# Two elementwise products of an RWKV-6 and MLP-mixer kernel, given from VectorE to GpSimd

## The chip, the cores and the metric

The kernel runs on one core of one Trainium2 chip. A core has five engines with a queue of instructions each: TensorE (PE in the profile; its weight loads are PEld), VectorE (DVE), ScalarE (ACT), GpSimd (POOL) and SyncE (SP), which here issues the DMAs. The metric is the time of one execution on the device in microseconds; the median of three runs before the change is 521.4 us (519.96 to 521.54).

## The reference

A linear recurrence over 768 time steps feeds a token mixer and a channel mixer, all in float32. Batch B = 4, heads H = 8, steps S = 768, head size D = 48.

```python
for t in range(S):                                   # attention block
    cur = np.einsum('bhd,bhe->bhde', u[None] * kt, vt)
    y[:, :, t] = np.einsum('bhd,bhde->bhe', rt, state + cur)
    state = wt[:, :, :, None] * state + np.einsum('bhd,bhe->bhde', kt, vt)
x = y.transpose(0, 2, 1, 3).reshape(B, S, H * D)
h = np.maximum(x.transpose(0, 2, 1) @ w_tok1, 0.0) @ w_tok2      # 768 -> 256 -> 768
z = x + h.transpose(0, 2, 1)
out = z + np.maximum(z @ w_ch1, 0.0) @ w_ch2                     # 384 -> 1536 -> 384
```

What matters for the change is the term with `u`: a step's own key counts in its own output, weighted by `u`. For a step and a head it is one number, the sum over the 48 places of a head of r times k times u.

## The kernel before, in words

The recurrence is worked in chunks of 64 steps. A *unit* is 256 steps of one batch for all heads; there are twelve (three for each batch). In a unit, VectorE forms running products of the decays by scans (`ends`, line 372, and `begins`, line 380), scales the keys (`keys`, line 377) and the queries (`queries`, line 383) with them; TensorE transposes the keys (`k_ps`, line 287), multiplies keys by queries to the weights of steps within a chunk (`gram`, line 257), makes each chunk's contribution to the state (`kv_ps`, line 303) and the outputs (`y_ps`, line 317 for what comes from the state and line 338 for what comes from within the chunk). VectorE masks the gram into the tile `at` (line 425) and advances the state (line 448), ScalarE scales the state (line 438).

The diagonal of `at`, a step's weight on itself, is made apart. Units 0 to 3 make it on TensorE. Units 4 to 11 make it from rows of tokens: a DMA (line 154) brings r and k of the unit's 256 steps side by side as the tile `near`, 128 partitions by 2 by (2 x 384); `products` multiplies r by k in place (line 400), then by `u` (line 402, `u_rows` holds u in all partitions), then sums over each head's 48 places (line 405); `sums_put` writes the 16 sums of a partition on the diagonal of `at` by a predicated copy (line 410), before the second part of `y_ps` is made. `near` has one buffer: the next unit's load follows the reduction of line 405 in the queue of SyncE, and waits for it.

The mixer of one batch is interleaved with the units of the next. The token mixer is `h_ps` (lines 522 and 529) with a transpose (line 537). The channel mixer's first product is made in blocks of 256 tokens, as fifteen products of thirds (`thirds`: `z_ps`, line 585, gathered by ScalarE at line 590, by VectorE at lines 593, 596 and 599, and cut at zero by ScalarE at line 602); its second product in seven products of halves (`quarters`: `q_ps`, lines 642 and 646, gathered at lines 655 to 684, with sums of `z` at lines 689 and 690). For the first batch plain products take the place of some of these (lines 547 and 624).

The order of work is written out by hand. `woven` merges lists of steps by their weights, and the function `strict` then binds the instructions of TensorE, VectorE, ScalarE and, in part, SyncE to that order, each within its own engine's queue. GpSimd is not among the engines so bound; before the change it has only a few memsets and selects at the start, and a load and branches at the end. The dependencies between engines are semaphores that the framework puts in from the tiles read and written.

In the middle batches the three steps of `products` are woven with the first ten steps of `thirds`, in the function `middle_mixing`; in the first mixing they stand one by one between the steps of the unit, in `steps`.

Of the kernel before, what the change touches and what calls it, by code (L numbers as in the profile page):

```python
# [20 lines left out]
DM = H * D  # L21
T = 64
C = S // 128
UC = 2
# [38 lines left out]
def rwkv6_then_mixer(  # L63
# [18 lines left out]
    pe, dve, act, pool, sp = nc.tensor, nc.vector, nc.scalar, nc.gpsimd, nc.sync  # L82
# [35 lines left out]
    u_rows = const.tile([128, DM], f32, name="u_rows")  # L118
# [227 lines left out]
    def unit(i):  # L346
# [50 lines left out]
        def products(n):  # L397
            t = nears[i]
            if n == 0:
                dve.tensor_mul(t[:, :, 0], t[:, :, 0], t[:, :, 1])  # L400
            elif n == 1:
                dve.tensor_mul(t[:, :, 0], t[:, :, 0], u_rows.unsqueeze(1).to_broadcast([128, UC, DM]))
            else:
                L["sums"] = apool.tile([128, UC, H], f32, name="sums")
                dve.tensor_reduce(out=L["sums"], in_=nears.pop(i)[:, :, 0].rearrange("p c (h e) -> p c h e", e=D),
                                  axis=mybir.AxisListType.X, op=ALU.add)
# [58 lines left out]
        def each(f, n):  # L465
            return [lambda m=m: f(m) for m in range(n)]

        return dict(ranges=each(ranges, 2), ends=ends, keys=keys, begins=begins, queries=queries, own_u=each(own_u, A),
                    own_gram=own_gram, copied=each(copied, UC), taken=each(taken, 3),
                    own_put=own_put, products=[lambda n=n: products(n) for n in range(3)], sums_put=sums_put,  # L470
                    tokens=tokens, gram=gram, mask=mask, carry=carry, before=before, seen=seen, after=after,
                    scaled=[lambda c=c, j=j: scaled(c, j) for c in range(UC) for j in range(2)],
# [354 lines left out]
    for bt in range(B):  # L827
        ahead = []
        if bt == 0:
            to_ch = [single(e, n) for n, e in enumerate(to_ch)]  # L830
            both = [f for e in zip(ups[0], ups[1]) for f in e]
            b, t = [turned[0]] + turned[1:10:2], turned[2:12:2] + turned[11:]
# [127 lines left out]
```

## Time and profile before

| | |
|---|---|
| median of three runs | 521.4 us |
| the profiled execution's own time | 518.61 us |
| its span, first to last instruction | 516.9 us |
| granted TensorE clock, mean | 0.989 |
| TensorE busy | 490.1 us (95%) |
| VectorE busy | 388.4 us (75%), 633 instructions |
| ScalarE busy | 229.2 us (44%) |
| GpSimd busy | 1.3 us, 10 instructions |
| near loads, line 154 | 8 of 768 KB, 4.1 to 5.6 us from issue to landing |

The span is what the profile covers, and the profiled execution's own time is 1.7 us longer; that execution was quicker than the median of the three runs. Busy times are sums over one engine's instructions and say nothing alone on what sets the end: the chain of waits does, and the idle time of an engine that is named there.

### The profile page before, as it was taken

How to read it: one execution, taken by the hardware profiler on the slowest of the kernel's cores; microseconds unless marked ns; L12 is line 12 of the kernel's file. 1: busy time of each engine (PE TensorE's matmuls, PEld its weight loads, DVE VectorE, ACT ScalarE, POOL GpSimd, SP SyncE). 2: the span in 40 equal slices, each digit the busy share in tenths (PEclk: the TensorE clock that was granted, in tenths of full speed). 3: DMA queues.
4: the chain of work that ended last, by engine and by line, in shares of the span. 5: the costliest groups of instructions: out<-in, count | busy, mean ns of one | idle time of the engine just before them, and what ended most of it. 6: DMA issues, size and time to landing. Idle time of an engine off the chain costs nothing.

```text
span 516.9 us, 13327 instructions
## 1 busy us (share of the span) xinstructions
PE 490.1 (95%) x5794; PEld 427.7 (83%) x5794; DVE 388.4 (75%) x633; ACT 229.2 (44%) x533; POOL 1.3 (0%) x10
## 2 busy tenths in 40 slices
PE   3589999899999999999999999999999999999996
PEld 2476687666789768999999868999999859999996
DVE  7999969959895878967779668987858616684653
ACT  3967675564453435434325445524335414531300
POOL 0000000000000000000000000000000000000000
PEclk9789999999999999999999999999999999999999
DMA  8845954443342442121212522100000000000000
GB/s 298 324 168 163 276 176 149 155 152 93 115 113 79 149 134 62 63 73 63 70 54 64 164 74 63 61 33 0 3 32 1 18 15 1 1 2 34 1 32 34
DMA packets 20946, 46.06 MB, mean 89 GB/s; under 512 B 2129, under 2 KB 13009, under 8 KB 20881
## 3 DMA queue, kind: packets, MB, share of 16 engines
q1 hardware_dynamic: 20736, 45.14, 27.6%
q8 instruction: 47, 0.77, 0.6%
q14 instruction: 19, 0.15, 0.1%
q10 hardware_dynamic: 144, 0.00, 0.0%
HBM read 40.41 MB, written 4.72 MB: 87 GB/s over the span
## 4 chain that ended last, share of the span: by engine, by line
PE 74%; DVE 16%; ACT 5%; issue 3%; DMA 1%; DVEq 0%
PE z_ps L585 18%; PE q_ps L646 12%; PE q_ps L642 11%; PE h_ps L529 6%; PE h_ps L522 6%; PE h_ps L624 5%; PE z_ps L547 3%; PE gram L257 2%; PE y_ps L317 2%; PE y_ps L338 2%; DVE w L380 2%; DVE to_end L372 2%; PE kv_ps L303 2%; PE xT_ps L537 2%; DVE z L593 2%
## 5 line engine op out<-in xcount | busy, mean ns | idle before, releaser
L438 ACT ACTIVATE before<-state,to_end 112x48 f32<-112x48 f32 x176 | 44.5, 324 | 65.0 <-DVE state L448 60.7
L590 ACT COPY z<-z_ps 128x512 f32<-128x512 f32 x54 | 30.6, 587 | 57.4 <-PE z_ps L585 39.5
L593 DVE TENSOR_TENSOR z<-z,z_ps 128x512 f32<-128x512 f32 x54 | 35.9, 683 | 24.5 <-PE z_ps L585 15.9
L547 PE MATMUL z_ps<-xT,wch 128*128 128x256 f32 x216 | 48.3, 381 | 0.9 <-DVE wch L227 0.9
L602 ACT ACTIVATE z<-z 128x512 f32<-128x512 f32 x54 | 33.3, 631 | 33.1 <-DVE z L593 29.0
L547 PEld LDWEIGHTS z_ps<-xT,wch 128*128 128x128 f32 x216 | 40.4, 190 | 6.9 <-DVE wch L227 1.3
L646 PE MATMUL q_ps<-wch,z 128*128 128x192 f32 x222 | 43.3, 331 | 0.0
L642 PE MATMUL q_ps<-wch,z 128*128 128x192 f32 x222 | 42.8, 329 | 0.2
L642 PEld LDWEIGHTS q_ps<-wch,z 128*128 128x128 f32 x222 | 36.5, 190 | 0.9 <-ACT z L602 0.6
L646 PEld LDWEIGHTS q_ps<-wch,z 128*128 128x128 f32 x222 | 36.5, 190 | 0.6
L529 PE MATMUL h_ps<-h,wtok 128*128 128x384 f32 x96 | 34.9, 492 | 0.6 <-ACT h L524 0.6
L596 DVE TENSOR_TENSOR z<-z,z_ps 128x512 f32<-128x512 f32 x45 | 30.0, 683 | 7.0 <-PE z_ps L585 6.5
L624 PE MATMUL h_ps<-wch,z 128*128 128x384 f32 x96 | 33.3, 494 | 1.4 <-DVE wch L227 1.4
L522 PE MATMUL h_ps<-x,wtok 128*128 128x384 f32 x96 | 33.1, 491 | 0.0
L531 DVE TENSOR_TENSOR x<-x,h_ps 128x384 f32<-128x384 f32 x24 | 13.2, 551 | 24.4 <-PE h_ps L529 24.4
L585 PE MATMUL z_ps<-rk,wch 128*128 128x128 f32 x256 | 31.2, 275 | 0.0
L585 PEld LDWEIGHTS z_ps<-rk,wch 128*128 128x128 f32 x256 | 30.0, 192 | 0.0
L372 DVE TENSOR_TENSOR_SCAN to_end<-w,starts 112x1041 f32<-112x1041 f32 (+1 forms) x13 | 28.1, 2159 | 2.1 <-DMA w<-in_w_dram 1.7
L380 DVE TENSOR_TENSOR_SCAN w<-w,starts 112x1041 f32<-112x1041 f32 x12 | 27.8, 2320 | 0.0
L624 PEld LDWEIGHTS h_ps<-wch,z 128*128 128x128 f32 x96 | 17.5, 190 | 12.4 <-DVE wch L227 2.0
L646 PE MATMUL q_ps<-scratch,z 128*128 128x192 f32 x144 | 27.7, 329 | 0.0
L642 PE MATMUL q_ps<-scratch,z 128*128 128x192 f32 x144 | 27.4, 327 | 0.0
(181 smaller groups left out, 912.6 us busy)
## 6 DMA issues: line engine op xcount, KB each, us to landing
rk<-in_rk_dram SPq DMA_DIRECT2D x36, 192.0 KB, 3.7
near<-in_near_dram SPq DMA_DIRECT2D x8, 768.0 KB, 4.3
w<-in_w_dram SPq DMA_DIRECT2D x11, 520.5 KB, 3.7
vt<-in_v_dram SPq DMA_DIRECT2D x12, 384.0 KB, 3.8
out_dram<-o SPq DMA_DIRECT2D x24, 192.0 KB, 1.9
spare<-in_w_ch_dram SPq DMA_DIRECT2D x8, 512.0 KB, 4.9
scratch<-in_w_ch_dram SPq DMA_DIRECT2D x8, 512.0 KB, 4.8
rk<-in_rk_dram SPq DMA_DIRECT2D x6, 512.0 KB, 8.5
```

The source lines that it names most:

```text
L372: dve.tensor_tensor_scan(to, of, start, 0.0, op0=ALU.mult, op1=ALU.add)
L380: dve.tensor_tensor_scan(w_[:ROWS], w_[:ROWS], starts[:ROWS], 0.0, op0=ALU.mult, op1=ALU.add)
L438: act.mul(t[:ROWS, a], state[bt, g][:ROWS, a], by_last(c, j)[:, a:a + 1])
L522: pe.matmul(sums[i], wtok1[:, c, ts(i, 128)], x_of()[:, c, :], start=(c == 0), stop=(c == C - 1))
L529: pe.matmul(ps, wtok2[:, i, ts(c, 128)], h1[:, i, :], start=(i == 0), stop=(i == DTOK // 128 - 1))
L547: pe.matmul(ps, wch1[:, m, ts(jt, 128)], xT[:, m, ts(s, SEG)], start=(m == 0), stop=(m == DM // 128 - 1))
L585: pe.matmul(ps[:, q], lefts[r][:, ts(q, 128)], of[r], start=first and q == 0, stop=end and q == JB - 1, skip_group_check=True)
L593: dve.tensor_add(to(n), to(n), ps)
L602: act.activation(to(n), to(n), AF.Relu)
L624: pe.matmul(ps, zs[s][:, jt, ts(n, 128)], wch2[:, jt, :], start=(jt == 0), stop=(jt == NJ - 1))
L642: pe.matmul(L["q"], a[:, j, :], b[:, j, :], start=(j == 0), stop=False)
L646: pe.matmul(L["q"], a[:, j, :], b[:, j, :], start=False, stop=(j == HJ - 1))
```

## The change

The two products of `products` are issued on GpSimd rather than on VectorE, for units 4 to 11. The reduction of line 405 stays on VectorE.

```diff
         def products(n):
             t = nears[i]
             if n == 0:
-                dve.tensor_mul(t[:, :, 0], t[:, :, 0], t[:, :, 1])
+                pool.tensor_mul(t[:, :, 0], t[:, :, 0], t[:, :, 1])
             elif n == 1:
-                dve.tensor_mul(t[:, :, 0], t[:, :, 0], u_rows.unsqueeze(1).to_broadcast([128, UC, DM]))
+                pool.tensor_mul(t[:, :, 0], t[:, :, 0], u_rows.unsqueeze(1).to_broadcast([128, UC, DM]))
             else:
                 L["sums"] = apool.tile([128, UC, H], f32, name="sums")
                 dve.tensor_reduce(out=L["sums"], in_=nears.pop(i)[:, :, 0].rearrange("p c (h e) -> p c h e", e=D),
                                   axis=mybir.AxisListType.X, op=ALU.add)
```

VectorE's queue has 16 instructions fewer, GpSimd's 16 more, in the order of the units; the other queues keep their instructions and their order. In GpSimd's queue the first product of a unit waits for the near load and for the earlier readers of the tile, the second for the first (in unit 4 also for the load of `u_rows`, line 722), and the reduction on VectorE now waits for GpSimd.

## Prediction

> **What bounds the kernel now.** I read the engines' shares first, then the chain that ended last, then what TensorE waited for in the stretch where the eight units run, and last the timeline around each near load.
>
> ```profile
> PE 490.1 (95%) x5794; PEld 427.7 (83%) x5794; DVE 388.4 (75%) x633; ACT 229.2 (44%) x533; POOL 1.3 (0%) x10
> ...
> PE 74%; DVE 16%; ACT 5%; issue 3%; DMA 1%; DVEq 0%
> ```
>
> The first line is the busy time of the engines, the second the chain by engine. TensorE is busy for 95% of the span and carries 74% of the chain; VectorE has a quarter of its time free. Of the chain's pieces from 100 to 430 us, none is at line 400 or 402. The reduction of line 405 is in it three times (165.4, 238.0 and 355.9 us), but it stays on VectorE. So the question is where TensorE waits for VectorE. The waits of TensorE's matmuls between 126 and 430 us are two lines:
>
> ```profile
> PE y_ps L317 <- ACT before L438: 0.6, 1, 0.6
> PE gram L257 <- DVE rk L383: 0.3, 2, 0.2
> ```
>
> The columns are the total in us, the number and the longest. In 304 us TensorE stands idle for 0.9 us. Nothing that makes VectorE faster here can give back more than that.
>
> **What is removed.** The two groups that leave VectorE, and the rows of GpSimd that come nearest to what it gets, by form:
>
> ```profile
> L402 DVE TENSOR_TENSOR near<-near,u_rows 128x768 f32<-128x768 f32 x8 | 7.6, 951 | 0.0
> L400 DVE TENSOR_TENSOR near<-near 128x768 f32<-128x768 f32 x8 | 7.6, 949 | 0.0
> ```
>
> ```profile
> L177 POOL TENSOR_SCALAR_AFFINE_SELECT strictly<-strictly 64x64 f32<-64x64 f32 x2 | 0.5, 236 | 0.1
> masks.py:199 POOL TENSOR_SCALAR_AFFINE_SELECT ident<-ident 128x128 f32<-128x128 f32 x1 | 0.3, 294 | 0.1
> ```
>
> VectorE loses 16 instructions of 0.95 us, 15.2 us of 388.4. Most of them ran into a wait of VectorE for somebody else: after line 400 at 229.44 it waits 2.42 us for z_ps, after line 402 at 160.25 0.58 us for q_ps, at 183 the later 0.87 us for h_ps. In the stretches without such a wait (203 to 207, 321 to 325 us) TensorE runs its thirds' products without a gap, so an earlier VectorE only waits longer. Gain taken: 0; bound: 0.9 us.
>
> **What GpSimd gets.** Eight times two products of 768 elements a partition, two operands from SBUF. The trace has no such instruction on GpSimd, so the price is bounded. From 64 to 128 elements the select grows by 58 ns, 0.91 ns an element over a base of 178 ns, reading one tile and writing one. At that slope 768 elements take 0.87 us, the low end. If the second operand is read after the first, the slope doubles: 178 + 768 x 1.81 = 1.57 us, which I take, as that is the select's row with one read more. If the write does not overlap either, three times the slope: 2.27 us, the high end.
>
> A page of the Trainium skill (GPSIMD Engine Reference, section 3.1) gives 4497 ns for a two-operand product of 2048 elements against 2293 ns on VectorE. An estimate from it is 1.69 us for 768, and the sum below would be some 0.5 us larger.
>
> **When it runs, and who waits.** GpSimd's queue is not under the hand-written order; its first product of a unit waits for the near load alone (and the tile's earlier readers), so it starts when the load lands, not where VectorE stood. Landings, from issue and time to landing, against the reduction that needs the result: 110.0/138.3, 144.6/165.3, 170.4/184.9, 190.3/206.9, 212.1/237.9, 243.1/269.6, 274.9/324.8, 330.1/355.8. The closest pair is 14.5 us apart, and two products at the high end with a hand-over take under 5 us. (The first unit's second product waits for u_rows, issued at 108.84 and landed 2.4 us later.) So the new wait of the reduction on GpSimd costs 0; if it did come late, the update of line 448 behind it, and the scaling and the product y_ps after it, would be next. Nothing else is in GpSimd's queue until the end, and the queue on SyncE keeps its order: the next near load still follows the reduction, at 184.9 and 206.9 up to 1.7 us earlier, as VectorE has less to do in front of it.
>
> **What it disturbs.** The trace shows no VectorE instruction with two SBUF operands beside a running GpSimd one (GpSimd's ten all lie in the first 2.1 us, beside a memset). The one end is that both run undisturbed, cost 0. The other is that VectorE stands still as long as GpSimd runs. I take the step between: one of the two waits for the other where both read two tiles in SBUF, and not where VectorE reads PSUM, since GpSimd touches no PSUM tile here.
>
> The Trainium skill (SBUF — State Buffer, "Who interferes with whom") says the same and speaks against this change: a VectorE instruction with two SBUF inputs and a GpSimd one that reads SBUF share a read interface, and the one that comes second blocks for the whole of the first; no run shown here can tell. Without it, only the odds between the ends would be more even.
>
> Site by site, two products of 1.57 us from the landing on. At 110 VectorE idles (4.70 us before line 628): 0. At 144.6 the weight sums and a scan are held by some 2.5 us, but keys (line 377) end at 149.7 for a transpose at 154.4, and 3.43 us of idle follow: 0. At 190.3 the predicated copy at 193.05 slips by under 1 us, with 2 us in hand before y_ps at 196.4; at 212 and 330 line 377 slips by under 1.5 us, with 4 us in hand; at 243 2.07 us of idle follow: 0 each. Two places are left.
>
> The first is at 275 us:
>
> ```profile
> 275.43 1.22 DVE L377 TENSOR_TENSOR rk<-rk,to_end 112x1024 f32<-112x1024 f32 x1
> ...
> 277.56 0.36 DVE L656 TENSOR_TENSOR o<-x,z 128x192 f32<-128x192 f32 x1 [0.91 <-ACT z L655]
> ...
> 277.84 2.32 DVE L380 TENSOR_TENSOR_SCAN w<-w,starts 112x1041 f32<-112x1041 f32 x1
> ...
> 282.06 1.22 DVE L383 TENSOR_TENSOR rk<-rk,w 112x1024 f32<-112x1024 f32 x1
> ...
> 283.33 1.26 PE L257 MATMUL gram<-rk 48*64 48x64 f32 x64 [0.17 <-DVE rk L383]
> ```
>
> Every line from 277.56 on is in the chain, and TensorE already waits at its end. With the load landed at 274.85, the first product runs from 274.95 to 276.52; line 377 starts 1.09 us late and ends at 277.74; the second product runs to 279.31; line 656 starts there instead of at 277.56, and all that follows is 1.75 us late. At 0.87 us a product it is 0.35, at 2.27 us 3.15.
>
> The second is at 170.4 us: the predicated copy (170.69) waits until 172.05, the second product runs from 173.25 to 174.82, line 673 starts at 174.82 instead of 172.26. Of these 2.56 us the waits of VectorE for q_ps (0.18 and 1.68) take most: the scan of the next unit starts 0.55 late, and with it keys, for which the transpose at 180.8 already waits: 0.5 us. By the ends of the price 0 and 2.
>
> Sum: 1.75 + 0.5 = 2.25 us on the profiled execution's span of 516.9 (its own time is 518.61). The median of the runs is 521.4, which gives 523.65, 0.43% more. With the ends of the price it is +0.35 to +5.15.
>
> **Rivals.** *No collision* (0.31): both engines read at once; VectorE is 15 us less busy, TensorE gets at most the 0.9 us back: 520.5 to 521.4. For it: nothing in the trace shows a shared thing. It decides if a VectorE product beside a GpSimd one keeps its 0.95 us. *VectorE stands still at every landing* (0.14), PSUM reads too: of 3.14 us at each, what the slack leaves is 1.3 at 170, 2.0 at 190, where y_ps already waits for before, 1.0 at 212 and 330, 1.1 at 243 and 2.2 at 275: +8.6, about 530. *The relief reaches TensorE by a way that the chain hides* (0.05), say a PSUM bank freed earlier: over 1.6 us, below 519.8; against it stand the 0.9 us. The likeliest case, my forecast, has 0.5.
>
> **Numbers.** A measurement of this kernel tells about 0.3%, 1.6 us, from no change. The forecast case passes that with some 0.36 of its 0.5 (a product over about 1.3 us); with the standstill, slower is 0.50. No collision and the rest make 0.45 within it, and 0.05 is faster. The range goes from 520.5 (all idle given back) to 526.5 (the forecast's upper end); most of the standstill and the hidden relief are left out, under 2 in 10. The forecast's own range is 521.7 to 526.5.
>
> **What would show it.** GpSimd has 16 products of 1.2 to 2 us, each pair begun within 0.5 us of a landing; VectorE's busy time falls by 15 us less what its rows beside them grow by; lines 377 and 380 near 275 us, or line 410 near 171, last longer or start later; gram waits near 283 us for line 383 by about 2 us rather than 0.2. The twin place near 400 us, with no load before it, stays as it is. It is wrong if those VectorE rows keep their times (no collision), if rows that read PSUM grow as well (standstill), or if a reduction waits for GpSimd.

## The result and the profile after

The changed kernel is slower: a ratio of 1.0049 to the kernel before, 95% interval 1.0039 to 1.0059, which is 2.5 us. Over 19 runs each the medians are 521.73 us after and 519.32 us before; the 521.4 us that the prediction started from was the median of three runs only, so the difference is to be compared, not the absolute time. The profiled execution of the changed kernel has a span of 520.0 us against 516.9, at a granted TensorE clock of 0.99.

The engines' busy time and the chain by engine, page of the changed kernel:

```profile
PE 491.6 (95%) x5794; PEld 428.3 (82%) x5794; DVE 386.0 (74%) x617; ACT 229.2 (44%) x533; POOL 38.7 (7%) x26
...
PE 72%; DVE 18%; ACT 4%; issue 4%; DMA 1%; SPq 0%; DVEq 0%; ACTq 0%
```

VectorE has 16 instructions fewer and yet is busy only 2.4 us less, and its share of the chain has grown from 16% to 18%. What TensorE's matmuls waited for between 126 and 434 us (total, number, longest, in us):

```profile
PE gram L257 <- DVE rk L383: 1.1, 2, 1.0
PE k_ps L287 <- issue: 0.8, 1, 0.8
PE y_ps L317 <- ACT before L438: 0.6, 1, 0.6
PE k_ps L287 <- DVE rk L377: 0.5, 1, 0.5
```

0.9 us of waits have become 3.0: line 383 is waited for longer, and the matmuls of the keys' transpose (`k_ps`), which are not in the table of before, wait for line 377 once by name (at 181.92) and once under "issue", where the profile names nobody: that one begins at 279.21, 0.1 us after line 377's end.

The place near 275 us in the timeline (start, length, instruction, idle time before it), GpSimd and VectorE:

```profile
276.12 0.68 DVE L596 TENSOR_TENSOR z<-z,z_ps 128x512 f32<-128x512 f32 x1
276.20 1.83 POOL L400 TENSOR_TENSOR near<-near 128x768 f32<-128x768 f32 x1 [28.18 <-DVE z L593]
...
276.72 2.39 DVE L377 TENSOR_TENSOR rk<-rk,to_end 112x1024 f32<-112x1024 f32 x1
...
278.10 2.95 POOL L402 TENSOR_TENSOR near<-near,u_rows 128x768 f32<-128x768 f32 x1
...
279.03 0.34 DVE L656 TENSOR_TENSOR o<-x,z 128x192 f32<-128x192 f32 x1
...
279.30 3.94 DVE L380 TENSOR_TENSOR_SCAN w<-w,starts 112x1041 f32<-112x1041 f32 x1
...
286.41 1.26 PE L257 MATMUL gram<-rk 48*64 48x64 f32 x64 [0.96 <-DVE rk L383]
```

Line 377 took 1.22 us before and 2.39 now: it ends about as long after the end of GpSimd's first product (278.03) as it needs for itself. GpSimd's second product is then the one that is held: its 2.95 us end at 281.05, 1.7 us after line 656 is over, and undisturbed it takes 1.81. And line 380, 2.32 us before and 3.94 now, waits for that: it ends 2.2 us after the product. Each waits for the other's end. Just ahead, at 276.12, the subtraction of line 596, which reads PSUM, keeps its 0.68 us beside the same first product.

The second place, at 171 us, first two lines of the kernel before, then the changed one:

```profile
172.26 0.36 DVE L673 TENSOR_TENSOR o<-o,z 128x192 f32<-128x192 f32 x1
172.54 0.68 DVE L511 TENSOR_TENSOR wch<-wch,spare 128x512 f32<-128x512 f32 x1
```

```profile
170.83 3.11 POOL L400 TENSOR_TENSOR near<-near 128x768 f32<-128x768 f32 x1 [19.17 <-DVE z L690]
171.00 1.30 DVE L410 COPY_PREDICATED at<-diagonal,sums 128x1024 f32<-128x1024 uint8 x1
...
172.57 1.59 DVE L673 TENSOR_TENSOR o<-o,z 128x192 f32<-128x192 f32 x1
...
174.02 1.81 POOL L402 TENSOR_TENSOR near<-near,u_rows 128x768 f32<-128x768 f32 x1
174.08 2.30 DVE L511 TENSOR_TENSOR wch<-wch,spare 128x512 f32<-128x512 f32 x1
...
181.92 1.09 PE L287 MATMUL k_ps<-ident,rk 128*128 128x128 f32 x8 [0.51 <-DVE rk L377]
```

Here the predicated copy keeps its time and GpSimd's first product is held behind it, although its recorded start is 0.17 us earlier: its end, 173.94, less 1.81 us is 172.13, about the copy's end. Then line 673 (0.36 us before) and line 511 (0.68 before) are held behind a product each.

A ledger comes from laying the start times of VectorE's instructions of the two timelines side by side (after minus before, in us):

| stretch | lag at its end | added in it |
|---|---|---|
| up to 54, ahead of the first product | 0.30 | 0.30 |
| unit 4's and 5's products, to 170 | 0.31 | 0.01 |
| unit 6's, to 188 | 1.04 | 0.73 |
| unit 7's and 8's, to 238 | 1.04 | 0.00 |
| unit 9's, to 260 | 1.29 | 0.25 |
| unit 10's, to 295 | 3.09 | 1.80 |
| unit 11's, to the end | 3.10 | 0.01 |

The products account for 2.8 us, at three places out of eight. The 0.30 us arise before any product; in the traces of the experiments this early lag is anything from -0.4 to 2.95 us, and it belongs to no theory.

### The profile page after: what moved, and what is told of

Its sections match the earlier page's. It is cut to its first block, busy times and chain, and to the rows that moved or that the text cites. A ratio compares the mean times of both kernels' runs of the same rounds, so it can differ in the third digit from the quotient of the medians.

```text
span 520.0 us, 13349 instructions
## 1 busy us (share of the span) xinstructions
PE 491.6 (95%) x5794; PEld 428.3 (82%) x5794; DVE 386.0 (74%) x617; ACT 229.2 (44%) x533; POOL 38.7 (7%) x26
## 4 chain that ended last, share of the span: by engine, by line
PE 72%; DVE 18%; ACT 4%; issue 4%; DMA 1%; SPq 0%; DVEq 0%; ACTq 0%
PE z_ps L585 18%; PE q_ps L646 12%; PE q_ps L642 11%; PE h_ps L529 6%; PE h_ps L624 5%; PE h_ps L522 5%; PE z_ps L547 3%; PE gram L257 3%; DVE w L380 2%; PE y_ps L317 2%; PE y_ps L338 2%; DVE to_end L372 2%; PE kv_ps L303 2%; PE xT_ps L537 2%; DVE rk L377 1%
## 5 line engine op out<-in xcount | busy, mean ns | idle before, releaser
L400 POOL TENSOR_TENSOR near<-near 128x768 f32<-128x768 f32 x8 | 17.4, 2170 | 300.0 <-DMA near<-in_near_dram 207.3
L372 DVE TENSOR_TENSOR_SCAN to_end<-w,starts 112x1041 f32<-112x1041 f32 (+1 forms) x13 | 29.5, 2271 | 2.1 <-DMA w<-in_w_dram 1.7
L380 DVE TENSOR_TENSOR_SCAN w<-w,starts 112x1041 f32<-112x1041 f32 x12 | 29.4, 2453 | 0.0
L646 PE MATMUL q_ps<-scratch,z 128*128 128x192 f32 x144 | 27.8, 329 | 0.0
## 6 DMA issues: line engine op xcount, KB each, us to landing
w<-in_w_dram SPq DMA_DIRECT2D x11, 520.5 KB, 3.9
```

The source lines that it names most:

```text
L372: dve.tensor_tensor_scan(to, of, start, 0.0, op0=ALU.mult, op1=ALU.add)
L380: dve.tensor_tensor_scan(w_[:ROWS], w_[:ROWS], starts[:ROWS], 0.0, op0=ALU.mult, op1=ALU.add)
L646: pe.matmul(L["q"], a[:, j, :], b[:, j, :], start=False, stop=(j == HJ - 1))
```

## The experiments

The theory is that GpSimd's reads of SBUF and VectorE's instructions with two SBUF operands exclude each other for a whole instruction, and that this costs only where TensorE soon waits for the VectorE instruction that was held. The rivals: the cost is the same for each product; it comes from the new wait of the reduction; any work of GpSimd disturbs; VectorE's relief is worth something that the collisions hide. In the edits, `dve` and `pool` are VectorE and GpSimd; the lines with a plus come in, in place of the two products unless it is said otherwise, and `...` marks what lies between. Lines behind an edit are a few numbers off.

**Relief alone.**

```diff
+            if n < 2:
+                return
```

> Neither engine makes the two products of line 400 and 402 (the diagonal's sums are then sums of the loaded r): what VectorE's relief alone is worth. My theory (TensorE bounds, idle 0.9 us in the stretch): no gain to speak of, 0 to 0.5 us under the kernel before, ratio 0.999 to 1.000. Rival (the relief of 13 to 15 us on VectorE is worth something that the collision hides): over 1 us under the kernel before, ratio under 0.998.

Measured: 0.9999 (0.9984 to 1.0015). VectorE is busy 374.7 us, 13.7 less than before, and TensorE's waits in the stretch are the same 0.6 and 0.3 us as before. The relief is worth nothing that can be measured, and the collisions in the changed kernel cost VectorE 386.0 - 374.7 = 11.3 us of busy time, of which 2.8 reach the end.

**Only units 6 and 10 on GpSimd.**

```diff
+            t, by = nears[i], pool if i in (6, 10) else dve
...
+                by.tensor_mul(t[:, :, 0], t[:, :, 0], t[:, :, 1])
...
+                by.tensor_mul(t[:, :, 0], t[:, :, 0], u_rows.unsqueeze(1).to_broadcast([128, UC, DM]))
```

> Only units 6 and 10 have their products on GpSimd, the other six on VectorE. Theory (the cost comes from the two places where a near load lands amid VectorE products on the chain, 0.7 us after 171 and 1.8 us at 276): +2.5 us over the kernel before, ratio 1.0048, as much as all eight. Rival (each GpSimd product costs the same, or the wait of the reduction on GpSimd does): two eighths of 2.8 us, +0.7 us, ratio 1.0013.

Measured: 1.0059 (1.0040 to 1.0078); by its trace, reckoned as in the ledger, 0.73 us are added at 171 and 1.84 at 276, and nothing elsewhere. Two units cost as much as eight. An even price per product falls, and a price on the reduction's wait with it.

**All but unit 10 on GpSimd.**

```diff
+            t, by = nears[i], dve if i == 10 else pool
...
```

and both products by `by`, as above.

> Units 4 to 9 and 11 on GpSimd, unit 10 on VectorE as before. Theory: the 1.8 us of the place at 276 us go, 0.7 and 0.25 stay: +1.0 us over the kernel before, ratio 1.002; line 377 and 380 there back to 1.2 and 2.3 us. Rival (even cost): seven eighths of 2.8, +2.4 us, ratio 1.0047.

Measured: 1.0012 (0.9997 to 1.0026). By its trace the place at 276 us adds nothing; lines 377 and 380 are back:

```profile
276.39 1.22 DVE L377 TENSOR_TENSOR rk<-rk,to_end 112x1024 f32<-112x1024 f32 x1
...
278.80 2.32 DVE L380 TENSOR_TENSOR_SCAN w<-w,starts 112x1041 f32<-112x1041 f32 x1
```

The interval takes in no change at all; it excludes the even price's 1.0047.

**GpSimd writes, but does not read.**

```diff
+            if n < 2:
+                for _ in range(2):
+                    pool.memset(t, 0.0)
```

> In place of each product GpSimd writes zeros over the whole near tile twice (the diagonal becomes zero): at 0.81 ns an element by the memset rows some 1.3 us each, 5.4 us a unit, at the same landings, reading nothing. Theory (what collides is the reading of SBUF by both): VectorE's lines 377 and 380 near 276 us keep 1.2 and 2.3 us, and the time is that of the kernel before within 0.4 us, ratio 0.999 to 1.001. Rival (any work of GpSimd holds VectorE's SBUF instructions up): +3 us or more, ratio over 1.005, with these rows over 2 and 3.5 us.

Measured: 1.0000 (0.9987 to 1.0012). The group of the memsets, and the timeline at the same place:

```profile
L401 POOL MEMSET near<- 128x1536 f32 x32 | 44.1, 1378 | 291.2 <-DMA near<-in_near_dram 134.1 <-ACT before L437 110.1 <-DVE z L592 25.4
```

```profile
276.39 5.69 POOL L401 MEMSET near<- 128x1536 f32 x4 [25.99 <-DMA near<-in_near_dram]
276.93 1.22 DVE L377 TENSOR_TENSOR rk<-rk,to_end 112x1024 f32<-112x1024 f32 x1
...
279.33 2.32 DVE L380 TENSOR_TENSOR_SCAN w<-w,starts 112x1041 f32<-112x1041 f32 x1
```

GpSimd works longer than in the changed kernel (45.4 us against 38.7) and covers lines 377 and 380 wholly (its four memsets run from 276.39 to 282.08); both keep their times. What collides is the reading.

**One operand on GpSimd.**

```diff
+            if n < 2:
+                pool.tensor_scalar(t, t, 2.0, None, op0=ALU.mult)
```

> In place of each product GpSimd doubles the whole near tile, 1536 elements, with one operand read from SBUF (the products are left out): by the select's rows (178 ns and 0.91 ns an element) some 1.6 us, about as long as a product. Theory A (any reading of SBUF by GpSimd collides with VectorE's two-operand instructions): +2 to +3 us over the kernel before, ratio 1.004 to 1.006, line 377 near 276 us over 2 us. Theory B (it takes two operands on GpSimd's side too): these rows keep 1.2 and 2.3 us and the time is that of the kernel before within 0.4 us.

Measured: 1.0336 (1.0299 to 1.0372), far more than expected, because the instruction took 4.1 us undisturbed (two in 8.26 us at 110 us) and not 1.6. At the same place:

```profile
285.44 8.50 POOL L400 TENSOR_SCALAR near<-near 128x1536 f32<-128x1536 f32 x2 [25.89 <-DMA near<-in_near_dram]
```

```profile
285.99 3.73 DVE L377 TENSOR_TENSOR rk<-rk,to_end 112x1024 f32<-112x1024 f32 x1
...
289.92 5.33 DVE L380 TENSOR_TENSOR_SCAN w<-w,starts 112x1041 f32<-112x1041 f32 x1
```

Lines 377 and 380 are held by 2.5 and 3.0 us: one operand read by GpSimd is enough, as theory A has it. The expected size was wrong because the instruction's price was. One thing is left open: here the held lines go on some 1.0 us before the multiply's recorded end (the first multiply ends at 289.52, and line 377's end, 289.72, less its 1.22 us is 288.50), where it is 0.1 us with the products. So the multiply held them for about 3 of its 4.1 us, and no run tells why.

**A third product in unit 10, beside the two.**

```diff
+                if i == 10:
+                    pool.tensor_mul(t[:, :, 1], t[:, :, 1], t[:, :, 1])
```

> As the changed kernel, and in unit 10 alone GpSimd makes a third product (k by k into k, which nobody reads afterwards), right behind the second, with VectorE's chain on the end's path. Theory: it takes the place of one more VectorE instruction on the chain, +1.5 to 1.8 us on top of the changed kernel's 2.6, ratio 1.008 against the kernel before; one of lines 689 or 383 after 283 us grows by 1.5 us. Rival (the 1.8 us there come from the wait or the hand-over and not from GpSimd's length): as the changed kernel, 1.005.

Measured: 1.0100 (1.0078 to 1.0121). In the trace the place at 276 us adds 2.9 us in place of 1.8. The instruction that pays was misjudged, though: line 658 (line 656 before the edit) is now held to 1.96 us, and the scan of line 380 to 3.58, by the second and the third product; 689 and 383 keep their times:

```profile
280.32 1.96 DVE L658 TENSOR_TENSOR o<-x,z 128x192 f32<-128x192 f32 x1
282.03 1.58 POOL L404 TENSOR_TENSOR near<-near 128x768 f32<-128x768 f32 x1
282.21 3.58 DVE L380 TENSOR_TENSOR_SCAN w<-w,starts 112x1041 f32<-112x1041 f32 x1
```

The trace gives 1.1 us for the third product, the ratios 1.0100 - 1.0049, 2.6 us with more than 1 us of doubt; both say that the cost grows with GpSimd's length. The difference between the two is open.

**The load of unit 10 issued later: two runs whose edit did not move it.** The piece that issues the load was set behind unit 9's load of w, in the second run with units 6 and 9 back on VectorE too.

> As the changed kernel, but the near load of unit 10 is issued in unit 9 behind the load of w, at about 305 us instead of 272, and lands near 310 us, where VectorE reads PSUM. Theory: GpSimd makes the same products and the place at 276 us is as before the change; 0.7 and 0.25 us stay: +1.0 us over the kernel before, ratio 1.002. Rival (the cost lies in GpSimd's work itself, wherever it falls): 1.005 as the changed kernel.

> Units 6 and 9 on VectorE, the other six on GpSimd, and the load of unit 10 moved as in the run beside it, so that no pair of products falls on VectorE's chain. Theory: the time of the kernel before, ratio 0.999 to 1.001, and no gain, since TensorE's waits stay 0.9 us. Rival (what VectorE is spared is worth something once nothing collides): under 0.998.

Measured: 1.0059 (1.0039 to 1.0079) and 1.0041 (1.0028 to 1.0054). In both the load was issued where it had been (at 270.70 us in the second): SyncE's queue is not under the written order in this part, and the load stayed right behind unit 9's reduction, for which it waits (269.73 + 0.95 us in the second). So the first is the changed kernel once more, and in the second only unit 10's collision reaches TensorE: its trace adds 1.7 us at 276 us and nothing that lasts elsewhere.

**The load held by a dependency.**

```diff
+            if i == 10:
+                dve.memset(nears[i][:, 0, 0, 0:1], 0.0)
             sp.dma_start(nears[i], near[i - UB - 1])
```

with the call of `load_near(10)` moved from behind unit 9's reduction to behind its `queries`, both in the changed kernel.

> The load of unit 10 held back by a dependency, since its place in the code alone did not move it: VectorE clears one column of the tile behind the queries of unit 9 (one more memset, under 0.1 us, at some 303 us), and the load must wait for that; it lands near 308 us, where VectorE's next instructions read PSUM. All eight units on GpSimd. Theory: at 276 us VectorE's lines 377 and 380 are back to 1.2 and 2.3 us; 0.8 and 0.25 us of the other two places stay: +1.0 us over the kernel before, ratio 1.002. Rival (the cost lies in GpSimd's work, wherever it falls): 1.005.

Measured: 1.0026 (1.0007 to 1.0044). GpSimd makes all sixteen products, unit 10's at 311 us; at 277 us its lines 379 and 382 (377 and 380 before the edit) take 1.22 and 2.32 us. By its trace 0.74 and 0.22 us are added at the other two places, and nothing that lasts at unit 10's:

```profile
276.62 1.22 DVE L379 TENSOR_TENSOR rk<-rk,to_end 112x1024 f32<-112x1024 f32 x1
...
279.02 2.32 DVE L382 TENSOR_TENSOR_SCAN w<-w,starts 112x1041 f32<-112x1041 f32 x1
...
310.75 1.82 POOL L402 TENSOR_TENSOR near<-near 128x768 f32<-128x768 f32 x1 [62.84 <-DVE at L427]
...
311.87 1.87 DVE L412 COPY_PREDICATED at<-diagonal,sums 128x1024 f32<-128x1024 uint8 x1
312.65 2.74 POOL L404 TENSOR_TENSOR near<-near,u_rows 128x768 f32<-128x768 f32 x1
```

The predicated copy is held there too (1.87 us, 1.30 undisturbed), but idle time of VectorE follows and takes it up. The same work of GpSimd costs 1.8 us at one place and nothing 34 us later.

> Units 6 and 9 on VectorE, the load of unit 10 held back as in the run beside it, six units on GpSimd with no landing on VectorE's chain. Theory: the time of the kernel before, ratio 0.999 to 1.001. Rival (GpSimd's help pays once nothing collides): under 0.998.

Measured: 1.0002 (0.9992 to 1.0012). With units 6 and 9 on VectorE and the load held, six units' products on GpSimd cost nothing and bring nothing. No version beat the kernel before.

## Why the prediction was right

**TensorE bounds, and VectorE's relief is worth 0.** Right: without any products the time is the same within 0.15%, and TensorE's 0.9 us of waits stay.

**GpSimd's price.** I took 1.57 us; undisturbed it is 1.81, in unit 7, where the VectorE instructions beside the products read PSUM:

```profile
189.43 1.81 POOL L400 TENSOR_TENSOR near<-near 128x768 f32<-128x768 f32 x1 [13.60 <-DVE x L531]
191.31 1.81 POOL L402 TENSOR_TENSOR near<-near,u_rows 128x768 f32<-128x768 f32 x1
```

The row of the select with a second read was a little low. The estimate by the Trainium skill (GPSIMD Engine Reference, section 3.1), 1.69, was nearer and low too; the page's row is for an add, not for a product. Six of the sixteen took longer than the 2 us foretold, 2.31 to 4.33, because VectorE held them.

**When it runs.** Right: each first product begins within 0.2 us of its load's landing (271.84 + 4.2 against 276.20 for unit 10). No reduction waits for GpSimd; the closest pair is unit 6's, 8 us apart, not the 14.5 less the products' length that I worked out, because the products were held and the reduction came earlier.

**What it disturbs.** Right in the main: VectorE instructions with two SBUF operands are held until a product's end (line 377 2.39 us in place of 1.22), those that read PSUM are not (line 596 0.68), and a GpSimd instruction that only writes holds nobody (lines 377 and 380 1.22 and 2.32 us beside the memsets). The step that was taken, that both engines must read two tiles, was too narrow: one operand on GpSimd's side is enough. The Trainium skill (SBUF — State Buffer, "Who interferes with whom"), which was weighed there, asks only that GpSimd reads SBUF, and the runs agree, but for the 1.0 us by which the multiply's record outlasts its hold. On who comes first the recorded starts do not settle it: at 171 us the product starts 0.17 us ahead of line 410 and goes behind it.

**The sum.** 275 us: 1.75 foretold, 1.80 measured, and the closeness is in part luck. The path was not the one described: line 656 slipped in ahead of the second product, and line 380 was held in its place. Along the path described, at the measured 1.81 us a product, the cost would have been 2.23 (an estimate: 276.76, 277.98 and 279.79 in place of 276.52, 277.74 and 279.31); a price that was too low and a path that was too dear nearly cancelled. And `gram` waits 0.96 us for line 383, not the 2 foretold: `k_ps` had waited 0.81 ahead of it. 171 us: 0.5 foretold, 0.73 measured; the working had line 410 held, but line 410 went first and the product waited, and VectorE paid at lines 673 and 511. 243 us: 0 foretold, 0.25 measured. The step that failed is "2.07 us of idle follow", by the price: two products of 1.57 us from 244.30 on would have ended by 247.5, ahead of line 656, but at 1.81 the second runs to 248.02 and holds that line, the state behind it, and so `y_ps`:

```profile
246.21 1.81 POOL L402 TENSOR_TENSOR near<-near,u_rows 128x768 f32<-128x768 f32 x1
...
247.63 0.60 DVE L656 TENSOR_TENSOR o<-x,z 128x192 f32<-128x192 f32 x1 [1.34 <-ACT z L655]
```

(Line 656 took 0.36 us at 246.59 before.) The other five places cost nothing, as worked out, although VectorE is held at some of them too: line 372 at 146 us takes 3.78 us in place of 2.33 and line 377 at 216 us 2.29 in place of 1.22, in front of idle time. The twin place near 400 us stays as it was, as foretold (line 377 1.22 us at 396.43).

Sum: 2.25 foretold, 2.78 in the ledger, 2.5 in the ratio. The absolute time fits less well: 521.73 us against 523.65, since the 521.4 to which the sum was added is 2.1 us above the median of 19. Taken by itself it lies close to the 520.5 to 521.4 of *no collision*; it is the difference, the rows and the experiments that decide.

**The rivals.** *No collision* is refuted by the rows above, *standstill* by line 596's 0.68 us and by the places at 190, 212 and 330 us, which it priced at 1 to 2 us each and which cost nothing, *hidden relief* by the run without products and by the last run.

## What to carry to other kernels

Ask of work that is moved to an idle engine what that engine shares with the one that is relieved, and where in time it will land: here the moved instruction starts when its data arrive, not where it stood, and two of eight arrivals carried nine tenths of the cost. Price the relief by the waits of the bounding engine, not by the busy time that goes: 13.7 us less on VectorE bought nothing. If such a move must be made, hold the load back by a dependency so that it falls beside instructions that read PSUM or ahead of idle time; here the order in the code alone did not do it.

## What the runs showed that was not expected

GpSimd's one-operand multiply by a constant was slower for each element than its two-operand product: 4.1 us for 1536 elements, 2.7 ns each, against 1.81 us for 768, 2.4 ns each; its memset of 1536 took 1.38 us. And the exclusion is mutual: GpSimd's longest product, line 402 at 335.67 us, took 4.33 us in place of 1.81:

```profile
335.56 1.22 DVE L377 TENSOR_TENSOR rk<-rk,to_end 112x1024 f32<-112x1024 f32 x1
335.67 4.33 POOL L402 TENSOR_TENSOR near<-near,u_rows 128x768 f32<-128x768 f32 x1
...
338.26 0.35 DVE L660 TENSOR_TENSOR o<-x,q_ps 128x192 f32<-128x192 f32 x1
338.53 2.28 DVE L689 TENSOR_TENSOR z<-z,z 128x768 f32<-128x768 f32 x1
```

VectorE had begun line 377 just ahead of it and went on from one instruction with two SBUF operands to the next; at 338.26 came line 660, which reads PSUM, and the product's end at 340.0 less its 1.81 us falls there. Line 689 behind it paid with 2.28 us in place of 0.95. In that place nobody waited for it.
